# One load's last 20 KB per row, spread unevenly over the DMA engines

## The chip, the cores and the metric

The kernel runs on 1 core of one Trainium2 chip. The metric is the device time of one execution in microseconds, the median of several runs. A profiled execution has its own time, and inside that a span, which reaches from the first to the last instruction of the program that the profile shows.

## The reference

One decode step of a transformer block with modulation from a condition, for a batch of 2 and a single new token. The width is 512, there are 32 heads of 128, and the caches of keys and values hold 4096 positions per head and batch entry, all in fp32. Cut to what is computed:

```python
mod = (silu(c) @ w_mod).reshape(2, 6, 1, -1)        # sa, ca, ga, sb, cb, gb
h = layernorm(x) * (1 + ca) + sa
q = (h @ wq) split into 32 heads
scores = einsum("bhqd,bhkd->bhqk", q, k_cache) * 128 ** -0.5
o = einsum("bhqk,bhkd->bhqd", softmax(scores), v_cache)
x = x + ga * (o @ wo)
h = layernorm(x) * (1 + cb) + sb
x = x + gb * (mish(h @ w1 + b1) @ w2)               # 512 -> 1376 -> 512
```

The two caches are 2 x 32 x 4096 x 128 x 4 bytes each, 268 MB together. All inputs together are a little under 300 MB, and each byte is used once.

## The kernel before

**Layout.** Everything that is read in bulk (keys, values, weights) is laid out beforehand as rows of 128 partitions. One head's keys are `[128, 8192]` floats, 32 KB for each of the 128 rows; one head's values come in two halves of 16 KB per row; a piece of `wq` or `wo` is 8 KB per row. `stream()` packs these pieces in a fixed order into 36 loads, numbered 0 to 35. Loads 1 to 31 are 64 KB per row (`ROW`), 8 MB each, and every one of them holds the keys of the head of the same number. Load 27 holds, in this order in each row: the second half of head 23's values (16 KB), head 27's keys (32 KB), piece 7 of `wq` (8 KB) and piece 5 of `wo` (8 KB). Loads 32 to 35 are smaller and cut into several transfers; the last one, 35, ends with the weights `w2` in four transfers.

**Buffers and queue.** A load goes to one of three buffers named `room`. `load(n)` (line 137) issues load n's transfers on SyncE's queue, at line 143. `used()` issues load n as soon as everything in load n - 3 has been used, so that up to three loads are held or on their way. SyncE's issuing instruction waits for the semaphores of the work that used the buffer; the transfers themselves are queued on the 16 DMA engines behind those issued before. Each transfer has one of eight semaphores in turn.

**Work on a load.** For each head h, VectorE multiplies the keys in place by the query (`products`, line 320, 128x8192) and sums over 128 (`sums`, line 323). A row maximum, an exponential on ScalarE (`soft_max`) and the product with the values on TensorE (`weighted_v`, line 361) follow. `project_q` (line 293) makes the queries of four heads from a piece of `wq`, and `project_o` (line 392) adds four heads' values through a piece of `wo`. The order of these on each engine is the order of the loop over heads: the kernel's schedule is written by hand, and only the waits are put in by the framework.

**The end.** After the loop stand the last heads' values, the attention's output, the second layer norm, `w1`, the activation, and the product with `w2` (line 558) chunk by chunk as `w2` lands. Two VectorE instructions (lines 565 and 566) form `y`, which is stored at line 567.

Of the kernel before, what the change touches and what calls it, by code (L numbers as in the profile page):

```python
# [13 lines left out]
P = 128  # L14
# [11 lines left out]
OUT_STEP = 1  # L26
AHEAD = (14, 22)
ROW = 2 * BIG


def stream():


    order, n_v = [], 0
    for h in range(1, HEADS):
        order.append(("k", h))
        if h % HC == HC - 1 and HC < h < HEADS - 1:
            c = (h + 1) // HC
            order.append([("wq", c), ("wo", c - 2)])
        if h not in AHEAD:  # L40
            order += [("v", n_v, 0), ("v", n_v, 1)]
            n_v += 1
    order = [x if isinstance(x, list) else [x] for x in order]

    def size(x):
        return sum(SIZES[key[0]] for key in x)

    loads = [[([("m01", 0), ("wq", 0), ("wq", 1)], (4 * W,)), ([("k", 0)], (BIG,))]]
    for _ in range(1, HEADS):
        row = []  # L50
        while size(row) < ROW:
            room = ROW - size(row)
            row += order.pop(next(i for i, x in enumerate(order) if size(x) <= room))
        loads.append([(row, (ROW,))])
    last = [("v", h, i) for h in range(HEADS - 4, HEADS) for i in range(2)]
    assert order == [[key] for key in last[:2]], order
    loads += [
        [(last[:2] + [("wo", 6), ("wo", 7), ("m2", 0)], (BIG + 3 * W,))],
        [(last[2:4], (BIG,)), (last[4:6], (BIG,))],
        [([("m4", 0)] + last[6:], (W + HALF, W, W))],  # L60
        [
            ([("m3", 0), ("w1", 0)], (W + 2 * sum(WIDTHS), 2 * sum(WIDTHS))),
            ([("m5", 0), ("w2", 0)], (W + 5 * 512, 4 * 512, 512, 512)),
        ],
    ]
    return loads
# [3 lines left out]
def kernel(  # L70
# [17 lines left out]
    nc = tc.nc  # L88
# [29 lines left out]
    def take(t, keys):  # L118
        lo = 0
        for key in keys:  # L120
            kind, n = key[:2]
            part = t[:, lo : lo + SIZES[kind]]
            lo += SIZES[kind]
            if kind == "k":
                k_t[n] = part.rearrange("p (j d) -> p j d", d=DH)
            elif kind == "v":
                v_t[n, key[2]] = part.rearrange("p (c n) -> p c n", n=512)
            elif kind in ("wq", "wo"):
                (wq_t if kind == "wq" else wo_t)[n] = part.rearrange("p (k n) -> p k n", k=G)
            else:  # L130
                w_t[kind] = part.rearrange("p (k n) -> p k n", k=NCH if kind == "w2" else G)
# [4 lines left out]
    def load(n):  # L136

        t = kvp.tile([P, ROW], F32, tag="room", name=f"room{n}", bufs=3)
        lo = 0
        for keys, srcs in loads[n]:  # L140
            take(t[:, lo:], keys)
            for src in srcs:
                nc.sync.dma_start(out=t[:, lo : lo + src.shape[-1]], in_=src)  # L143
                lo += src.shape[-1]

    loaded = 0

    def used(*keys):

        nonlocal loaded  # L150
        done.update(keys)
        while loaded < len(loads) and (
            loaded < 3 or all(key in done for keys, _ in loads[loaded - 3] for key in keys)
        ):
            load(loaded)
            loaded += 1
# [16 lines left out]
        out=fold, in_=ident.rearrange("p (g r) -> p r g", g=G), axis=AX.X, op=ALU.add  # L173
# [3 lines left out]
        out=mean_w, in0=fold[:, None, :].to_broadcast([P, G, R]), scalar1=1.0 / D, scalar2=None, op0=ALU.mult  # L177
# [4 lines left out]
        out=half, in_=ident.rearrange("p (b r) -> p r b", b=B), axis=AX.X, op=ALU.add  # L182
# [330 lines left out]
    for k in range(G):  # L513
        lo = 0
# [9 lines left out]
    lo = 0  # L524
    for g in reversed(range(G)):
# [3 lines left out]
        lo = hi  # L529
# [41 lines left out]
def _lay_out(np, a):  # L571


    def rows(w):

        return w.reshape(-1, P, w.shape[-1]).transpose(1, 0, 2)

    def q_rows(v):

        return v.reshape(2, 4, P).transpose(1, 0, 2).reshape(8, P)  # L580

    B, H, S, DH = a["A_k_cache"].shape
    kv = {
        kind: a[n].reshape(B, H, P // B, -1).transpose(1, 0, 2, 3).reshape(H, P, -1)
        for kind, n in (("k", "A_k_cache"), ("v", "A_v_cache"))
    }
    wq = rows(a["A_wq"]).reshape(P, 4, 8, 512).transpose(2, 0, 1, 3).reshape(8, P, -1)
    wo = a["A_wo"].reshape(8, 4, P, 512).transpose(0, 2, 1, 3).reshape(8, P, -1)
    wm = rows(a["w_mod"])
    w1 = rows(a["B_w1"])  # L590
    starts = np.cumsum((0,) + WIDTHS)
    b1c = np.zeros((P, 12), a["B_b1"].dtype)
    w2 = np.zeros((P, len(CHUNKS), 512), a["B_w2"].dtype)
    for n, (g, j) in enumerate(CHUNKS):
        f0 = starts[g] + P * j
        f1 = min(f0 + P, starts[g + 1])
        b1c[: f1 - f0, n] = a["B_b1"][f0:f1]
        w2[: f1 - f0, n] = a["B_w2"][f0:f1]

    pieces = {**kv, "wq": wq, "wo": wo, "m01": [wm[:, :, :1024]], "w1": [w1], "w2": [w2]}  # L600
    for n in (2, 3, 4, 5):
        pieces[f"m{n}"] = [wm[:, :, 512 * n : 512 * (n + 1)]]
    def piece(kind, n, part=None):
        row = pieces[kind][n].reshape(P, -1)
        return row if part is None else row[:, HALF * part : HALF * (part + 1)]

    arrays = {
        "head": np.stack([q_rows(a["c"]), q_rows(a["A_x"])], axis=1),
        "b1c": b1c,
    }  # L610
    for n, parts in enumerate(stream()):
        for i, (keys, widths) in enumerate(parts):
            row = np.concatenate([piece(*key) for key in keys], axis=1)
            cuts = np.split(row, np.cumsum(widths)[:-1], axis=1)
            for j, t in enumerate(cuts):
                arrays[f"load{n}_{i}_{j}"] = np.ascontiguousarray(t)
    return arrays

# [27 lines left out]
```

## Time and profile before

| | |
|---|---|
| Time, median of 3 runs | 697.43 us (697.37 to 697.83) |
| The profiled execution's own time | 697.51 us |
| Its span | 695.7 us |
| Mean granted TensorE clock | 0.674 |
| Busy: VectorE, TensorE, ScalarE, GpSimd | 84%, 41%, 6%, 1% |
| DMA packets | 6802, 297.54 MB, mean 428 GB/s |

In the page and the answers of the trace, times are microseconds from the start of the span. PE is TensorE (PEld its weight loads), DVE is VectorE, ACT is ScalarE, POOL is GpSimd and SP is SyncE; a q behind the name means the engine's sequencer. In the view by windows, a row gives for each stretch the busy time and the number of instructions of each engine, then the granted clock, the share of the 16 DMA engines that were busy, and what they moved. A packet's whole time is counted in the window in which it begins, so that a share in a short window can be a little over 1.

### The profile page before, as it was taken

The page shows a single profiled execution, that of the slowest core. Times are in us where ns is not written, and L with a number is a line of the kernel's source. Part 1 is how long each engine was busy: PE and PEld are TensorE (multiplying, and loading weights), DVE is VectorE, ACT ScalarE, POOL GpSimd, SP SyncE. Part 2 cuts the span into 40 slices and gives each one's busy share as a digit, 9 for nine tenths or more (in the row PEclk, how much of TensorE's full clock was granted, in tenths as well). Part 3 has the DMA queues.
Part 4 walks back from the last instruction along what each step waited for, and adds up shares of the span by engine and source line. Part 5 has one row for each costly group of instructions (what it writes and reads, how often), then busy time and mean ns, then how long its engine had stood idle before and what let it go on. Part 6 is the DMA issues. An engine that isn't in the chain of part 4 may idle for free.

```text
span 695.7 us, 3912 instructions
## 1 busy us (share of the span) xinstructions
PE 284.7 (41%) x1636; PEld 103.9 (15%) x1636; DVE 587.5 (84%) x220; ACT 44.0 (6%) x168; POOL 4.2 (1%) x19
## 2 busy tenths in 40 slices
PE   3603334335145624335232806235333515124677
PEld 1201011001012201101100301011101101001235
DVE  3599989999999999999999999999999999899002
ACT  1000000000000000000000000000000010000011
POOL 2000000000000000000000000000000000000000
PEclk9855655669565566556585656666575568556899
DMA  9999999999999999999999999999999999999997
GB/s 387 458 422 422 422 457 445 419 423 430 437 453 422 426 430 427 456 430 419 430 437 452 427 422 426 445 434 437 426 423 442 430 448 427 422 434 423 423 420 297
DMA packets 6802, 297.54 MB, mean 428 GB/s; under 512 B 888, under 2 KB 1024, under 8 KB 1280
## 3 DMA queue, kind: packets, MB, share of 16 engines
q1 hardware_dynamic: 6624, 297.27, 99.1%
q8 instruction: 13, 0.21, 0.1%
q10 hardware_dynamic: 160, 0.01, 0.0%
q14 instruction: 5, 0.04, 0.0%
HBM read 297.22 MB, written 0.07 MB: 427 GB/s over the span
## 4 chain that ended last, share of the span: by engine, by line
DMA 69%; DVE 28%; PE 3%; issue 0%; SPq 0%; ACT 0%; DVEq 0%
DMA room<-in_load 69%; DVE room L320 14%; DVE s L323 14%; PE qps L293 1%; PE ov L361 1%; PE modps L249 1%; PE yps L558 0%; SPq L143 0%; DVE m L336 0%; DVE hcw L282 0%; PE hps L239 0%; ACT q L294 0%; DVE hq L272 0%; DVE hq L273 0%; DVE y L565 0%
## 5 line engine op out<-in xcount | busy, mean ns | idle before, releaser
L320 DVE TENSOR_TENSOR room<-room,q 128x8192 f32<-128x8192 f32 x32 | 278.1, 8691 | 46.8 <-DMA room<-in_load 39.6
L323 DVE TENSOR_REDUCE s<-room 128x64 f32<-128x8192 f32 x32 | 277.9, 8683 | 0.4 <-DVE m L336 0.3
L361 PE MATMUL ov<-room,e 128*32 128x512 f32 x1024 | 174.1, 832 | 74.2 <-ACT e L339 40.4
L332 PE MATMUL mt<-d,same 128*128 128x64 f32 x64 | 19.0, 393 | 200.0 <-DVE d L330 200.0
L361 PEld LDWEIGHTS ov<-room,e 128*32 128x32 f32 x1024 | 39.0, 144 | 181.8 <-issue 128.5
L339 ACT ACTIVATE e<-s,m 64x64 f32<-64x64 f32 x64 | 22.1, 345 | 553.8 <-DVE m L336 553.0
L293 PE MATMUL qps<-room,hcw 128*128 128x512 f32 x64 | 46.1, 891 | 4.8 <-DMA room<-in_load 4.0
L332 PEld LDWEIGHTS mt<-d,same 128*128 128x128 f32 x64 | 13.8, 268 | 228.0 <-DVE d L330 181.1
L347 PE MATMUL l<-l,ones 128*128 128x8 f32 x16 | 4.5, 358 | 76.4 <-ACT e L339 76.4
L384 PE MATMUL otp<-pick,o 128*128 128x8 f32 (+2 forms) x72 | 13.2, 311 | 33.7 <-ACT o L376 32.1
L293 PEld LDWEIGHTS qps<-room,hcw 128*128 128x128 f32 x64 | 17.9, 292 | 27.9 <-issue 21.9
L376 DVE COPY o<-ov 128x256 f32<-128x256 f32 x1 | 0.4, 425 | 24.1 <-ACT o L376 24.1
L384 PEld LDWEIGHTS otp<-pick,o 128*128 128x128 f32 x72 | 12.4, 259 | 42.7 <-ACT o L376 42.6
L347 PEld LDWEIGHTS l<-l,ones 128*128 128x128 f32 x16 | 3.8, 294 | 77.8 <-ACT e L339 77.8
L336 DVE TENSOR_REDUCE m<-mt 128x1 f32<-128x64 f32 x32 | 6.9, 217 | 6.3 <-PE mt L332 6.3
L339 ACT ACTIVATION_READ_ACCUMULATOR e<-s,m 64x1 f32 x64 | 11.8, 185 | 0.0
L392 PE MATMUL att<-room,ot 128*32 128x512 f32 x62 | 9.6, 676 | 5.2 <-DMA room<-in_load 4.7
L330 DVE TENSOR_SCALAR d<-half,m 128x64 f32<-128x64 f32 x32 | 8.1, 254 | 1.1
L249 PE MATMUL modps<-room,ct 128*32 128x128 f32 (+1 forms) x160 | 8.1, 346 | 2.1 <-DMA room<-in_load 2.1
L328 DVE TENSOR_REDUCE m<-s 128x1 f32<-128x64 f32 x32 | 6.9, 217 | 0.9
L376 ACT COPY o<-ov 128x512 f32<-128x512 f32 (+1 forms) x9 | 5.0, 561 | 27.7 <-PE ov L361 27.6
L294 ACT ACTIVATE q<-qps 128x512 f32<-128x512 f32 x8 | 4.8, 597 | 15.9 <-PE qps L293 15.7
(101 smaller groups left out, 61.2 us busy)
## 6 DMA issues: line engine op xcount, KB each, us to landing
room<-in_load SPq DMA_DIRECT2D x4, 4096.0 KB, 25.2
room<-in_load SPq DMA_DIRECT2D x1, 7168.0 KB, 38.9
room<-in_load SPq DMA_DIRECT2D x1, 3072.0 KB, 26.4
room<-in_load SPq DMA_DIRECT2D x3, 1024.0 KB, 28.5
room<-in_load SPq DMA_DIRECT2D x1, 2400.0 KB
room<-in_load SPq DMA_DIRECT2D x1, 2304.0 KB, 20.2
room<-in_load SPq DMA_DIRECT2D x1, 1376.0 KB, 15.6
room<-in_load SPq DMA_DIRECT2D x2, 256.0 KB, 22.6
```

Source lines behind the costliest of these rows:

```text
L249: nc.tensor.matmul(ps[R * g : R * (g + 1)], lhsT=ct[:, k, :], rhs=t[:, k, :].rearrange("p (m n) -> p m n", m=n)[:, :, P * g : P * (g + 1)] ...
L293: nc.tensor.matmul(ps, lhsT=hcw[:, k, :], rhs=wq_t[ch][:, k, :], start=(k == 0), stop=(k == G - 1))
L320: nc.vector.tensor_tensor(out=k_t[h], in0=k_t[h], in1=qv, op=ALU.mult)
L323: nc.vector.tensor_reduce(out=s_t[h], in_=k_t[h], axis=AX.X, op=ALU.add)
L328: nc.vector.tensor_reduce(out=m_t[h][:, 0:1], in_=s_t[h], axis=AX.X, op=ALU.max)
L330: nc.vector.tensor_scalar(out=d, in0=half, scalar1=m_t[h][:, 0:1], scalar2=None, op0=ALU.mult)
L332: nc.tensor.matmul(mps[h], lhsT=same, rhs=d, start=True, stop=True)
L339: nc.scalar.activation(e_t[i][own_b, :, M * i + 4 * b : M * i + 4 * b + 4], s_t[h][own_b].rearrange("p (c m) -> p c m", m=4), AF.Exp, bias ...
L347: nc.tensor.matmul(lps[n], lhsT=ones, rhs=sum_t[n % 2], start=True, stop=True)
L361: nc.tensor.matmul(ov[bank][R * g : R * (g + 1), :], lhsT=e_t[h % HC][:, NB // 2 * part + c, :], rhs=v_t[h, part][:, c, :], start=(first a ...
L384: nc.tensor.matmul(tps[:, x], lhsT=o_t[m], rhs=pick_t[n][:, m, x], start=(m == 0), stop=(m == 3),)
L392: nc.tensor.matmul(att[R * i : R * (i + 1), :], lhsT=ot_t[n % 2][:, i, :], rhs=wo_t[n][:, i, :], start=(n == 0), stop=(n == H // HC - (2 i ...
```

## The change

Load 27 is cut into two parts along each row: the first 44 KB (11264 floats) go as before, one transfer of 128 rows. The last 20 KB (5120 floats: the last 4 KB of head 27's keys, and the pieces of `wq` and `wo`) go as five transfers, all on the same queue and one behind the other:

- rows 0 to 111 in one transfer, 112 = 16 x 7 rows;
- rows 112 to 116, 117 to 121 and 122 to 126, a transfer of five rows each;
- row 127 in one transfer of five pieces of 4 KB, which the source holds as five rows of their own behind the 128 (padded with zeros that no transfer reads).

With seven rows for each of 16 engines in the first of these transfers and one row (or one piece) for each of five engines in the others, five of the 16 DMA engines carry 7 + 3 + 1/5 rows of 20 KB and the eleven others 7, where each carried 8 before. No byte is added or dropped. The instructions of the four computing engines are the same and in the same order; SyncE issues six transfers for load 27 in place of one. The first multiplication on head 27's keys (line 320) now waits for all six, since the last 4 KB of those keys lie in the part that is cut off; so does the projection of the queries at line 293, for the five that bring `wq`.

```diff
+MORE = 27
+PART = 5 * 1024
+EVEN = 112
...
-        loads.append([(row, (ROW,))])
+        loads.append([(row, (ROW - PART, PART) if len(loads) == MORE else (ROW,))])
...
             for src in srcs:
-                nc.sync.dma_start(out=t[:, lo : lo + src.shape[-1]], in_=src)
+                dst = t[:, lo : lo + src.shape[-1]]
                 lo += src.shape[-1]
+                if src.shape[0] == P:
+                    nc.sync.dma_start(out=dst, in_=src)
+                    continue
+                nc.sync.dma_start(out=dst[:EVEN], in_=src[:EVEN])
+                for r in range(EVEN, P - 1, 5):
+                    nc.sync.dma_start(out=dst[r : r + 5], in_=src[r : r + 5])
+                nc.sync.dma_start(
+                    out=dst[P - 1 :].rearrange("p (a b) -> p a b", a=5), in_=src[None, P:, : PART // 5]
+                )
...
+                if n == MORE and j:
+                    last = np.zeros((5, PART), t.dtype)
+                    last[:, : PART // 5] = t[-1].reshape(5, -1)
+                    t = np.concatenate([t, last])
                 arrays[f"load{n}_{i}_{j}"] = np.ascontiguousarray(t)
```

## The prediction

> **What bounds the kernel now.** I read the page first: its DMA queues (packets, MB, share of 16 engines), and the chain of work that ended last.
>
> ```profile
> span 695.7 us, 3912 instructions
> ...
> q1 hardware_dynamic: 6624, 297.27, 99.1%
> q8 instruction: 13, 0.21, 0.1%
> ...
> q14 instruction: 5, 0.04, 0.0%
> ...
> DMA 69%; DVE 28%; PE 3%; issue 0%; SPq 0%; ACT 0%; DVEq 0%
> ```
>
> The loads alone (q1) fill 99.1% of 16 engines' span. The kernel is bound by moving its bytes; VectorE's 28% of the chain is where the chain runs through the work that frees a buffer, while transfers already queued go on. The rate of one engine follows from the q1 row: 297.27 MB in 0.991 x 16 x 695.7 = 11,031 engine-us, 26.95 KB per us (thousands of bytes). A row of 20 KB (20,480 B) takes one engine 0.76 us.
>
> Can all 16 be always full and yet something be won? Only where they don't finish together. The view by windows at the end shows that:
>
> ```profile
> core 0: us, PE busy (x) PEld busy (x) DVE busy (x) ACT busy (x) POOL busy (x), PEclk, DMA share, GB/s
> ...
> 688.50:689.00 0.50, 0.00 (x0) 0.00 (x0) 0.05 (x1) 0.00 (x0) 0.00 (x0) 1.00 0.98 389
> 689.00:689.50 0.50, 0.24 (x9) 0.27 (x13) 0.00 (x0) 0.00 (x0) 0.00 (x0) 1.00 0.76 299
> 689.50:690.00 0.50, 0.50 (x28) 0.50 (x23) 0.00 (x0) 0.00 (x0) 0.00 (x0) 1.00 0.71 283
> 690.00:690.50 0.50, 0.50 (x29) 0.50 (x23) 0.10 (x1) 0.00 (x0) 0.00 (x0) 1.00 0.61 238
> 690.50:691.00 0.50, 0.50 (x28) 0.50 (x21) 0.19 (x1) 0.00 (x0) 0.00 (x0) 1.00 0.40 156
> 691.00:691.50 0.50, 0.43 (x16) 0.16 (x8) 0.00 (x0) 0.00 (x0) 0.00 (x0) 1.00 0.27 102
> 691.50:692.00 0.50, 0.34 (x12) 0.34 (x16) 0.00 (x0) 0.00 (x0) 0.00 (x0) 1.00 0.27 102
> 692.00:692.50 0.50, 0.50 (x28) 0.50 (x24) 0.00 (x0) 0.00 (x0) 0.00 (x0) 1.00 0.19 70
> ```
>
> Times 16, the share is the number of engines still at work: all at 688.75, about eleven at 689.75, six at 690.75, four at 691.5, three at 692.25. Every engine gets the same rows from the loads, so the unequal finish must have another cause; apart from some KB at the start and the store at the end, the only other traffic is that of the instruction queues q8 and q14, 18 packets in all, 13 of them of 0.21 MB / 13 = 16 KB. They can't be spread evenly over 16 engines. So about five engines lead, by some 3.0 us (done at about 689.4, the last ones at about 692.4), seven come between, and four are last.
>
> That the last engines set the end shows in the tail of the chain:
>
> ```profile
> 669.27 22.34 DMA room<-in_load
> 691.61 0.04 issue
> 691.66 1.30 PE yps L558 x40
> 692.96 0.02 issue
> 692.97 0.47 PE yps L558 x8
> ```
>
> PE takes the chunks of w2 as they land (691.61, and again just before 692.97), and behind the last landing lies a fixed tail of 695.7 - 692.9 = 2.8 us. Whatever moves the slowest engine's last landing moves the end by as much. The sum is made against the profiled execution, 697.51 us with its span of 695.7; the median, 697.43, is 0.08 lower, so changes carry over as they stand.
>
> **The change, part by part.** What it does to the bytes: eleven engines lose one 20 KB row, -0.76 us; five get 10.2 rows for 8, 2.2 x 0.76 = +1.67 us. If nothing else happened and the five are those that lead by 3.0 us, they end 1.3 us ahead of the old end, the last ones 0.76 us ahead of it: a gain of 0.76 us at the very most, 0.11%. About 0.2% (1.4 us) is what a measurement of this kernel can tell from no change. A gain that could be told has no source in this change, since no engine that is last now loses more than one row.
>
> [...]
>
> What it adds on SyncE: five more issues.
>
> ```profile
> L143 SPq DMA_DIRECT2D room<-in_load x45: 327/328/533, 0.7 to 670.2; - x45
> L143 SPq EVENT_SEMAPHORE  x36: 17/17522/20702, 13.0 to 662.2; - x36
> ...
> DMA to landing us min/median/max: 12.2/40.5/59.3
> ```
>
> Each takes 0.33 to 0.53 us, 2.7 us at most, and SyncE stands 17.5 us (median) at its waits before the next load. Median time to landing is 40.5 us, of which a load's own transfer is half (8.39 MB at 16 x 26.95 KB per us is 19.5 us), so another whole load is queued ahead: free. Were that cover gone, the price would be the 2.7 us. Smaller packets: the view by windows gives the rate on the rows of 64 KB around load 27's last third, and on the rows of 8 to 32 KB later.
>
> ```profile
> 540.00:550.00 10.00, 3.28 (x5) 1.67 (x6) 8.60 (x4) 0.00 (x0) 0.00 (x0) 0.50 0.99 426
> 550.00:560.00 10.00, 7.36 (x34) 2.89 (x36) 10.00 (x3) 2.12 (x7) 0.00 (x0) 0.82 0.98 426
> ...
> 650.00:660.00 10.00, 5.60 (x34) 1.45 (x34) 0.57 (x3) 0.88 (x4) 0.00 (x0) 0.83 0.99 424
> ```
>
> 426 against 424: 0.5% at most, on the third of one load that is cut off (8 x 0.76 = 6.1 us) 0.03 us. I take 0.
>
> The added wait: L320 for head 27, and behind it everything on VectorE, stands until all six transfers are in. Before, it waited like this:
>
> ```profile
> 506.50 40.87 DMA room<-in_load
> 547.36 0.02 issue
> 547.39 8.69 DVE room L320
> ...
> 564.88 0.02 SPq L143
> ```
>
> And by the view of waits (us in total, times, longest):
>
> ```profile
> DVE room L320 <- DMA room<-in_load: 39.6, 29, 2.5
> ```
>
> VectorE already waits for DMA 1.4 us a head (39.6 / 29), so it follows the loads and nothing else; a load's last row later by x makes it x later once, and the next issue (load 30, at 564.88 before) by x, against the queued load of 19.5 us. It costs nothing at the end by itself.
>
> Now the part with no row of its own: **five engines writing five neighbouring rows at the same time.** Every bulk transfer of the trace has 128 rows, eight for each engine, and all engines run together at one flat rate of 26.95 KB per us. That flat rate can be the engine's own, or that of a way into SBUF which each engine has to itself as long as all 128 rows are written, eight rows to a way. The trace can't part the two, because in it they coincide. In the first case a five-row transfer takes 0.76 us and the sum is the one above. In the second, neighbours share a way that is already full with the next load's rows of the engine to which it belongs (DMA share 0.98 and 0.99 in the two windows above). Bounds: no sharing, 0; all five rows and that engine on one way, each at a sixth of the rate, 6 x 0.76 - 0.76 = 3.8 us per transfer, 11.4 us for three (the fourth, 4 KB pieces of one row, is a fifth of that and lies within the rounding). The value that I take is the middle, 5.7 us, since eight rows to a way mean that five neighbours are more likely to sit on one or two ways than on five. The five engines then end 1.67 + 5.7 = 7.4 us later than before. Their lead covers 3.0, and the end moves by +4.4 us: 697.43 + 4.4 = 701.8. They don't catch up, because from there to the end their queue is never empty. The 112-row transfer could suffer too, if an engine's seven rows are not among its usual eight; bounded by a doubling, 7 x 0.76 = 5.3 us; I take 0, by the 128-row loads, the nearest rows, and leave it to the upper part of the range.
>
> [...]
>
> **The rivals.** *The balance comes out.* The rate is the engine's own, the leading five are the right ones: -0.76 us, 696.7. For it: the share of about eleven at 689.75 means just five that have finished, and five are loaded. [...] The five have 3.0 - 1.67 = 1.33 us to spare: it holds as long as the three transfers together lose less than that, 0.44 us each, and turns to a loss that can be told at 1.33 + 1.4 = 2.7 us, 0.9 us each. *The wrong five.* No view names an engine. If one of the five is among the last four, it ends 1.67 us later: 699.1; if it is among the middle seven (about 1.5 us behind the leaders), it ends where the old last one did, at about 697.5. *A gain that shows,* below 696.0, needs something that I don't see; it is left for the unknown.
>
> **How the numbers follow.** Shared ways 0.60, balance 0.27, wrong five 0.08 (half of it slower by over 0.2%), unknown gain 0.05. Slower 0.60 + 0.04 = 0.64; same 0.27 + 0.04 = 0.31; faster 0.05. The time is that of the likeliest, 701.8. Its own range goes from 699.0, where it begins to be told, to 697.43 + 11.4 + 1.67 - 3.0 = 707.5. The range of all goes from the balance, with 0.1 us to spare, 696.6, to 706.5, which leaves out the very end of the bound and the unknown gain.
>
> **What would show it.** In the windows at 540 to 560 us the share should stay near 1 while the GB/s fall below the 426 of before, since packets that share a way take longer without the engines' standing idle. L320 for head 27 should start at about 553, not 547.4, and VectorE should wait for DMA that much longer, once. At the end, the taper should be turned round: eleven engines done early, and five alone at the last, a share of about 0.3 for some us before a last landing near 697. The forecast is wrong if the share falls from 1 to 0 within some 2.5 us and the tail of the chain stands where it was or 0.8 us earlier; then the rate is the engine's own. If the taper is long, but VectorE's wait at head 27 is not, the five are the wrong ones.

## The result, and the profile after

The kernel with the change takes 708.11 us (median of four runs, 707.67 to 708.99); the kernel before took 697.4 us on the same chip (697.37 to 697.83). The ratio is 1.0154, 95% interval 1.0136 to 1.0171: slower by 10.7 us. The forecast was 701.8 us with a range up to 706.5; the direction is right, the size is not. One run of one kernel below, `r112_16`, took 742.56 us in a slower state than all the others and is left out of every figure.

The page of the profile after (rows of the span, of the GB/s in 40 slices of 17.7 us, of the load queue and of the chain):

```profile
span 706.3 us, 3925 instructions
...
GB/s 387 445 416 464 427 413 434 453 417 423 461 419 427 442 434 420 431 453 417 434 449 423 428 449 423 419 439 445 419 425 332 331 423 438 443 415 424 424 419 264
...
q1 hardware_dynamic: 6792, 297.27, 98.9%
...
DMA 62%; DVE 33%; PE 3%; another core or an unknown queue 2%; issue 0%; SPq 0%; ACT 0%; DVEq 0%
```

The same 297.27 MB move in a span that is 10.6 us longer, and yet the queue's packets fill 98.9% of 16 engines' time, where they filled 99.1%. So the engines didn't stand idle: packets took longer. Two slices show where, 332 and 331, from 529.7 to 565.0 us. The view by windows there, in the columns of before (the last three are the clock, the share of the DMA engines and GB/s):

```profile
540.00:550.00 10.00, 0.69 (x2) 0.50 (x2) 5.71 (x3) 0.00 (x0) 0.00 (x0) 0.50 1.05 225
550.00:560.00 10.00, 0.30 (x1) 0.33 (x2) 0.41 (x1) 0.00 (x0) 0.00 (x0) 0.50 1.01 315
560.00:570.00 10.00, 7.57 (x24) 2.46 (x23) 10.00 (x3) 1.44 (x6) 0.00 (x0) 0.78 0.96 415
```

225 and 315 GB/s at a share of 1, where 426 stood twice. At 560 us it is over. VectorE's timeline for the multiplications of heads 27 and 28 (start, busy time, and in brackets the idle time before it and what ended it; line 320 of before is line 332 here), and the view of waits:

```profile
559.59 8.69 DVE L332 TENSOR_TENSOR room<-room,q 128x8192 f32<-128x8192 f32 x1 [13.80 <-DMA room<-in_load]
...
578.48 8.69 DVE L332 TENSOR_TENSOR room<-room,q 128x8192 f32<-128x8192 f32 x1 [0.87 <-DMA room<-in_load]
```

```profile
DVE room L332 <- DMA room<-in_load: 50.1, 29, 13.8
```

Head 27 starts 12.2 us later than before (559.59 for 547.39), with one wait of 13.8 us; head 28 waits 0.87 us, no longer than the three heads before 27 (1.0 to 1.4 us). In the chain of waits the same stretch has another name:

```profile
545.53 0.25 DVE d L342
545.78 13.51 another core or an unknown queue
...
559.59 8.69 DVE room L332
```

That piece is the 2% of the page's "another core or an unknown queue". With one core there is no other: VectorE's timeline above names the transfers of a load (`room<-in_load`) for the same idle time. The end, by windows:

```profile
699.50:700.00 0.50, 0.13 (x5) 0.16 (x9) 0.00 (x0) 0.00 (x0) 0.00 (x0) 1.00 0.52 197
700.00:700.50 0.50, 0.50 (x24) 0.50 (x23) 0.00 (x0) 0.00 (x0) 0.00 (x0) 1.00 0.33 123
700.50:701.00 0.50, 0.50 (x29) 0.50 (x22) 0.00 (x0) 0.00 (x0) 0.00 (x0) 1.00 0.13 53
701.00:701.50 0.50, 0.50 (x28) 0.50 (x22) 0.29 (x1) 0.00 (x0) 0.00 (x0) 1.00 0.08 33
...
702.00:702.50 0.50, 0.28 (x11) 0.24 (x12) 0.00 (x0) 0.00 (x0) 0.00 (x0) 1.00 0.07 25
...
703.00:703.50 0.50, 0.50 (x23) 0.29 (x12) 0.00 (x0) 0.00 (x0) 0.00 (x0) 1.00 0.14 33
```

Half of the engines are at work at 699.75 us (0.52); before, that stood between 690.25 (0.61) and 690.75 (0.40). So the middle of the taper moved by some 9 us: not only the five, but the engines that were to carry less are late. From 701 us on about one engine is alone (0.08 x 16 = 1.3). The tail of the chain follows the last landing, as before:

```profile
679.62 22.60 DMA room<-in_load
702.22 0.04 issue
702.27 1.30 PE yps L570 x40
703.57 0.02 issue
703.59 0.47 PE yps L570 x8
```

703.57 for 692.96: the last landing moved by 10.6 us and the end with it.

### The profile page after: what moved, and what is told of

The parts are those of the page before. It is cut to its first block, busy times and chain, and to the rows that moved or that the text cites. A ratio compares the mean times of both kernels' runs of the same rounds, so it can differ in the third digit from the quotient of the medians.

```text
span 706.3 us, 3925 instructions
## 1 busy us (share of the span) xinstructions
PE 285.1 (40%) x1636; PEld 105.1 (15%) x1636; DVE 587.5 (83%) x220; ACT 44.0 (6%) x168; POOL 4.2 (1%) x19
## 3 DMA queue, kind: packets, MB, share of 16 engines
q1 hardware_dynamic: 6792, 297.27, 98.9%
## 4 chain that ended last, share of the span: by engine, by line
DMA 62%; DVE 33%; PE 3%; another core or an unknown queue 2%; issue 0%; SPq 0%; ACT 0%; DVEq 0%
DMA room<-in_load 62%; DVE room L332 16%; DVE s L335 16%; PE qps L305 1%; PE ov L373 1%; PE modps L261 1%; PE yps L570 0%; SPq L149 0%; DVE m L348 0%; DVE d L342 0%; DVE hcw L294 0%; DVE m L340 0%; ACT q L306 0%; PE hps L251 0%
## 5 line engine op out<-in xcount | busy, mean ns | idle before, releaser
L396 PE MATMUL otp<-pick,o 128*128 128x8 f32 (+2 forms) x72 | 13.8, 319 | 35.9 <-ACT o L388 34.6
```

Source lines behind the costliest of these rows:

```text
L396: nc.tensor.matmul(tps[:, x], lhsT=o_t[m], rhs=pick_t[n][:, m, x], start=(m == 0), stop=(m == 3),)
```

## The experiments

The theory on record was that neighbouring rows share a way, so that the five-row transfers delay the five engines; its rivals were an engine's own rate (bytes alone), and the wrong five. The ways are the author's supposition (theory W below): the runs show how long packets take by the rows that are written, and none shows a way itself. After the result a third thing stood open: whether the 112-row transfer, priced at nothing, was slow too. Two families of kernels part them. Each run's ratio is against the kernel before, run on the same chip (697.42 to 697.52 us).

### The cut and its transfers of 16 engines

These start from the kernel before, cut load 27 as the change does, and bring the 20 KB in transfers of 128, 112, 64 or 16 rows, all multiples of 16, so that every engine is meant to get the same eight rows' worth (in the trace after, by its packets, the 112 rows went seven to each engine):

```diff
+MORE = 27
+PART = 5 * 1024
+PIECES = [(0, 128, 1)]                         # cut: first row, end, step
-        loads.append([(row, (ROW,))])
+        loads.append([(row, (ROW - PART, PART) if len(loads) == MORE else (ROW,))])
...
-                nc.sync.dma_start(out=t[:, lo : lo + src.shape[-1]], in_=src)
+                dst = t[:, lo : lo + src.shape[-1]]
+                for first, end, step in PIECES if n == MORE and src.shape[-1] == PART else [(0, P, 1)]:
+                    nc.sync.dma_start(out=dst[first:end:step], in_=src[first:end:step])
```

**The cut alone** (`cut`).

> Load 27 in two transfers of 128 rows, 44 KB and 20 KB wide: the cut alone, no other shape and no uneven split. Theory W (the rows of SBUF are reached over 16 ways, each as fast as one engine; a transfer of 128 rows gives every engine a way of its own, every other shape makes engines share): no change, 697.4 within 0.5 us, packets of 20 KB take 0.76 us. Theory T (a transfer costs by being small or cut off, wherever its rows lie): up to 1 us slower.

697.58 us, ratio 1.0002 (0.9992 to 1.0012). Its 20 KB packets took 0.76 to 0.77 us each (here and below, the times of single packets are from the trace's packet records). Windows:

```profile
540.00:560.00 20.00, 9.95 (x34) 4.92 (x34) 18.44 (x6) 1.95 (x6) 0.00 (x0) 0.67 1.05 452
```

No dip: the cut, the smaller packets and the added wait cost nothing.

**112 rows and 16 rows** (`r112_16`), without a five-row transfer.

```diff
+PIECES = [(0, 112, 1), (112, 128, 1)]
```

> The 20 KB as rows 0 to 111 and rows 112 to 127, so that every engine carries 7 + 1 = 8 rows as before: no uneven split and no five-row transfer. If the five-row transfers were the cost, as the prediction priced it, 697.4. [...]

705.98 us (median of three runs, 705.06 to 706.51), ratio 1.0121 (1.0104 to 1.0138).

```profile
540.00:560.00 20.00, 4.11 (x6) 2.01 (x7) 9.36 (x4) 0.00 (x0) 0.00 (x0) 0.50 1.00 261
```

With no engine meant to carry more than another and no five-row transfer, about 8.5 of the 10.7 us are there: 261 GB/s at a share of 1.00, the median 20 KB packet takes 1.50 us for 0.77.

**Eight transfers of 16 neighbouring rows** (`next16`).

```diff
+PIECES = [(0, 16, 1), (16, 32, 1), (32, 48, 1), (48, 64, 1), (64, 80, 1), (80, 96, 1), (96, 112, 1), (112, 128, 1)]
```

> The 20 KB as eight transfers of 16 neighbouring rows, one row for each engine in each. [...] Theory T: eight transfers cost the same here as with rows 8 apart.

711.45 us, ratio 1.0201 (1.0185 to 1.0216).

```profile
540.00:560.00 20.00, 0.69 (x2) 0.50 (x2) 5.87 (x3) 0.00 (x0) 0.00 (x0) 0.50 1.03 186
```

The slowest, with a median packet of 2.06 us, 2.7 times the usual. One such transfer costs about (711.45 - 697.58) / 8 = 1.7 us, so that of the 8.4 us between `r112_16` and `cut` some 6.7 belong to the 112 rows, if the two add up.

**Eight transfers of every eighth row** (`step16`).

```diff
+PIECES = [(0, 128, 8), (1, 128, 8), (2, 128, 8), (3, 128, 8), (4, 128, 8), (5, 128, 8), (6, 128, 8), (7, 128, 8)]
```

> The same eight transfers of 16 rows, one row for each engine, but each of every eighth row of 128. [...] Theory T: the same time as with neighbouring rows.

705.54 us, ratio 1.012 (1.0105 to 1.0135).

```profile
540.00:560.00 20.00, 4.68 (x7) 2.35 (x8) 9.94 (x4) 0.00 (x0) 0.00 (x0) 0.50 1.00 283
```

Spreading the same 16 rows over all partitions brings the median packet from 2.06 to 1.55 us and the loss from 13.9 to 8.0 us. Which rows are written together decides, not the number of transfers, which is eight in both: theory T, with the same time for the two, is out.

**Two halves of 64 rows** (`half64`).

```diff
+PIECES = [(0, 64, 1), (64, 128, 1)]
```

> The 20 KB as rows 0 to 63 and rows 64 to 127, four rows for each of 16 engines in each transfer. Theory W: 64 rows of one half lie on eight of the 16 ways, so two engines on each: 1.5 us a packet, 8 x 0.76 = 6 us slower, 703.5. Theory T: two transfers in place of one, under 1 us.

705.48 us, ratio 1.0116 (1.0101 to 1.0131).

```profile
540.00:560.00 20.00, 4.96 (x8) 2.40 (x9) 10.11 (x4) 0.00 (x0) 0.00 (x0) 0.51 1.00 281
```

Even two even halves double the packets (1.55 us, 1.55 / 0.77 = 2.0). The expectation had 1.5 us from two engines on a way; the time agrees, and the sharing itself is not shown. The 16 rows of `step16` have the same 1.55 us, the 16 neighbours of `next16` 2.06 us.

### Five engines by themselves, behind load 34

The other family leaves all loads of before as they are and appends three transfers of five rows of 20 KB behind load 34, into columns that nothing uses; load 35 follows as before, and what the three bring is never read. Five engines carry 3 x 0.76 = 2.28 us more, in rows that are chosen:

```diff
+EXTRA = [(112, 117, 1), (117, 122, 1), (122, 127, 1)]      # x_neigh
+WIDE = 5120
...
+        if n == 34:
+            spare, src = t[:, ROW - WIDE :], loads[1][0][1][0][:, :WIDE]
+            for first, end, step in EXTRA:
+                nc.sync.dma_start(out=spare[first:end:step], in_=src[first:end:step])
```

**The change's neighbouring rows** (`x_neigh`).

> The kernel before, and behind load 34 three transfers of five rows of 20 KB (rows 112 to 126, into columns of that buffer that nothing reads, the bytes read twice): five engines carry 3 rows more, 2.28 us, the other eleven what they had. Nothing else is cut. If the five lead by 3.0 us and share no way, no change. [...]

703.81 us, ratio 1.0091 (1.0074 to 1.0108); packets 1.23 to 2.22 us.

**Rows four apart, from 0** (`x_own`).

```diff
+EXTRA = [(0, 20, 4), (1, 20, 4), (2, 20, 4)]
```

> The same three extra transfers of five rows, but rows 0, 4, 8, 12, 16 and so on, four apart. [...] By the lead of 3.0 us no change, 697.4; if the slowest of the five leads by only 1.1 us, 698.6. Theory T: the same time as with neighbouring rows.

698.49 us, ratio 1.0015 (1.0006 to 1.0024); all 15 packets 0.76 to 0.77 us. The same bytes, again on five engines, cost 1.0 us here and 6.3 us there.

**Rows four apart, from 64** (`x_far`).

```diff
+EXTRA = [(64, 84, 4), (65, 84, 4), (66, 84, 4)]
```

> The same three extra transfers of five rows, four apart, but in the other half of the rows: 64, 68, 72, 76, 80 and so on. [...] Theory T: the same as the other two.

702.88 us, ratio 1.0083 (1.0066 to 1.01); packets 0.99 to 1.58 us, most of them 1.5. The rows lie four apart as in `x_own`, and yet they lose 5.4 us (702.88 for 697.46 of the kernel before) where those lose 1.0: the distance between the rows doesn't decide alone.

The three in one window, after the row of before:

```profile
670.00:680.00 10.00, 8.33 (x103) 4.47 (x95) 1.77 (x8) 1.40 (x4) 0.42 (x1) 1.00 1.02 427
```

`x_neigh`:

```profile
670.00:680.00 10.00, 5.34 (x46) 1.36 (x38) 0.00 (x0) 0.58 (x1) 0.00 (x0) 0.79 1.04 253
```

`x_own`:

```profile
670.00:680.00 10.00, 8.36 (x104) 4.59 (x96) 1.81 (x8) 1.40 (x4) 0.42 (x1) 1.00 1.02 428
```

`x_far`:

```profile
670.00:680.00 10.00, 8.10 (x59) 3.15 (x59) 0.42 (x1) 1.13 (x3) 0.08 (x1) 0.83 1.04 275
```

The share is above 1 in all; what the engines move falls from 427 to 253 and 275 GB/s, and stays at 428 in `x_own`.

**Is it the reading or the writing?** `x_own_src` writes rows four apart and reads the neighbouring ones, `x_neigh_src` the other way round (in each pair of triples the first is written, the second read):

```diff
+EXTRA = [((0, 20, 4), (112, 117, 1)), ((1, 20, 4), (117, 122, 1)), ((2, 20, 4), (122, 127, 1))]  # x_own_src: written, read
+EXTRA = [((112, 117, 1), (0, 20, 4)), ((117, 122, 1), (1, 20, 4)), ((122, 127, 1), (2, 20, 4))]  # x_neigh_src
```

> The extra transfers of five rows into rows four apart (0, 4, 8, 12, 16 and so on), but read from five neighbouring rows of the source (112 to 116 and so on). Theory W (the cost lies where the rows are written): as with rows four apart on both sides, 698.5, packets 0.76 us. Theory R (it lies where they are read from): as with neighbouring rows on both sides, 703.8, packets 1.2 to 2.2 us.

> The reverse: written to neighbouring rows (112 to 116 and so on), read from rows four apart (0, 4, 8, 12, 16). Theory W: 703.8, packets 1.2 to 2.2 us. Theory R: 698.5, packets 0.76 us.

698.53 us, ratio 1.0015 (1.0006 to 1.0024), and 703.23 us, ratio 1.0082 (1.0066 to 1.0099). First `x_own_src`, then `x_neigh_src`:

```profile
670.00:680.00 10.00, 9.43 (x101) 4.54 (x100) 1.01 (x4) 1.53 (x5) 0.42 (x1) 0.83 1.02 427
```

```profile
670.00:680.00 10.00, 5.07 (x43) 1.17 (x35) 0.00 (x0) 0.63 (x2) 0.00 (x0) 0.75 1.03 252
```

The rows that are written decide. For the transfers of 112, 64 and 16 rows the two sides were not exchanged.

**Rows four apart, from 32** (`x_own32`).

```diff
+EXTRA = [(32, 52, 4), (33, 52, 4), (34, 52, 4)]
```

> The extra transfers of five rows into rows 32, 36, 40, 44, 48 and so on, 32 above those of the kernel that cost nothing but its bytes. [...] Theory W with ways of eight neighbouring rows: 32, 36 and 40, 44 lie in pairs on one way each, beside another engine's rows: about 702, packets 1.5 us or more.

698.67 us, ratio 1.0016 (1.0007 to 1.0026), packets 0.76 to 0.77 us.

```profile
670.00:680.00 10.00, 8.14 (x100) 4.30 (x92) 1.81 (x8) 1.40 (x4) 0.42 (x1) 1.00 1.01 425
```

Rows 32 to 50 are as free as rows 0 to 18 (698.67 and 698.49 us, packets of 0.76 to 0.77 us in both), and rows 64 to 82 are not (702.88 us, most packets 1.5 us). Ways of eight neighbouring rows, by which about 702 us and 1.5 us were expected here, are ruled out.

**One extra transfer in its own rows** (`x_own1`), for the lead of the five:

```diff
+EXTRA = [(0, 20, 4)]
```

> One of the three extra transfers into rows 0, 4, 8, 12, 16: 0.76 us more for each of the five engines. If three of them cost 1.07 us because the slowest of the five leads by 2.28 - 1.07 = 1.2 us, one costs nothing: 697.4 within 0.3. If the cost is that of issuing, a third of it: 697.8.

697.55 us, ratio 1.0000 (0.999 to 1.0009). 0.76 us more on each of the five costs nothing, 2.28 us cost about 1.0: the slowest of the five leads the last engine by at least 0.76 us and by about 2.28 - 1.0 = 1.2 to 1.3 us, not by 3.0. The taper of `x_own` shows it:

```profile
693.00:693.50 0.50, 0.50 (x24) 0.50 (x20) 0.00 (x0) 0.00 (x0) 0.00 (x0) 1.00 0.07 25
693.50:694.00 0.50, 0.50 (x24) 0.35 (x16) 0.00 (x0) 0.00 (x0) 0.00 (x0) 1.00 0.17 37
```

0.07 of 16 is one engine, alone from 693 us on. Five with equal leads would end together, at 0.3.

Of theory W's expectations, `cut` (697.4), `x_own_src` (698.5) and `x_neigh_src` (703.8) came out within 0.6 us; `half64` came out 2.0 us above its 703.5. The theory leaves out the rows of other transfers: in the four kernels of the first family that lost time, 8 or 9 rows of the 44 KB part and 17 or 18 of load 28 were slowed too, in `cut` one and none.

## Why the prediction was right in its direction and wrong in its size

The last engine of the kernel after can be followed through its packets, since each begins within some ns of the end of the one before on the same engine. That is an inference from their times, as no view names the engine. In it:

```
                                       forecast     after
bytes, 2.2 rows x 0.76                   +1.67      +1.67
seven rows of the 112-row transfer        0         +5.4    (10.7 us for 5.3)
three five-row transfers                 +5.7       +2.65   (4.9 us for 2.27)
last row of the 44 KB part                0         +1.6
4 KB piece, first row of load 28          0         +0.6
lead of the five                         -3.0       -1.2    (from x_own)
sum                                      +4.4      +10.7    (measured +10.7)
```

- **The step that failed is the 112-row transfer, taken at 0.** The prediction gave it the bound of a doubling, 5.3 us, and then the value of the 128-row loads as the nearest rows. But by the prediction's own theory, eight rows to a way, those loads are the one case without sharing, so they could not price a transfer of another number of rows. The bound was the value: in the kernel after, 127 packets of 20 KB have a median of 1.47 us, and `r112_16` shows the loss without any five-row transfer. In the kernel after itself, 48 rows began and ended between 542.2 and 548.0 us, when nothing but the 112-row transfer was under way, and took 1.32 to 1.56 us each. All 16 engines paid it, which is why the whole taper moved: even the first engine to end load 28 did so at 571.96 us, for 563.95 before.
- **The five-row transfers, 5.7 us,** were about right as a number: `x_neigh` less `x_own` is 703.81 - 698.49 = 5.3 us. They were not right in kind, and that the number fits is luck: the forecast put the delay into the three rows of the five engines. In `x_neigh` three median packets (1.84 us) lose only 3 x (1.84 - 0.76) = 3.2 us; the rest must be lost in rows that were under way beside them, which took 2.5 to 2.7 times their usual time at 674.0 us. In the kernel after, the last engine lost 2.65 us in its three. No run shows the shared way from which the 5.7 us was worked out; what the runs show is the time of the packets by the rows written, 1.23 to 2.22 us in rows 112 to 126 (`x_neigh`) and 0.76 to 0.77 us in rows 0 to 18, four apart (`x_own`).
- **The rows under way beside these transfers** were not priced. The slowed stretch takes them in: 8 rows of the 44 KB part took up to 3.25 us (usually 1.67), and 36 rows of load 28 up to 5.42 us (usually 2.42). Some 2.2 us of it fall on the last engine.
- **The lead, 3.0 us,** is true of the five engines that finish first, but they are not the five that were loaded. In the packets of the kernel after, the five began their last row of the 44 KB part 0, 0.03, 0.12, 0.63 and 2.05 us behind the first of the 16: the fifth of them was the last of all. `x_own1` and `x_own` put the lead of the slowest at 1.2 us. This is the rival of the wrong five, in part. The bytes alone, 1.67 - 1.2, would have cost 0.5 us (an estimate), which could hardly be told.
- **That the balance comes out,** the first rival, is ruled out by `x_neigh`, `x_far` and `r112_16`. Five extra rows at a time cost nothing but their bytes in rows 0 to 18 and 32 to 50, four apart (`x_own` 698.49 us, `x_own32` 698.67 us). Whether all of load 27's last 20 KB could be written so, with the right five loaded, no run shows.
- **Right:** 0.76 us a row (0.76 to 0.77 in `cut`); five more issues, the small packets and the added wait at nothing (`cut`, and SPq 0% of the chain after); a share near 1 with fewer GB/s at 540 to 560 us; VectorE's single long wait at head 27, though to 559.59 and not 553; no catching up, since the last landing and the end moved together. The split came out as intended: by the packets of the trace after five of the 16 engines carry ten rows of 20 KB and a 4 KB piece and the eleven others seven.
- **The taper** is turned round only at its very end: one engine alone for two us (0.08 and 0.07), where five at 0.3 were forecast, because the eleven others were late as well.

## To carry to other kernels

Before work is moved between DMA engines, ask for each transfer which rows its engines write at the same moment: here only transfers of all 128 rows, and those of five rows four apart among rows 0 to 18 or 32 to 50, ran at the full rate (0.76 to 0.77 us for 20 KB), and transfers of 112, 64 or 16 rows about halved it or worse (medians of 1.47 to 2.06 us). A share of the DMA engines near 1 doesn't say that they work at their rate (1.05 at 225 GB/s above); read GB/s beside it. And where a forecast rests on a mechanism, put every transfer through it, not only the one that looks odd.

## What the runs showed of the hardware that was not expected

- **The other engines slow down too, not only the five that carry the extra rows.** In `x_far`, of the load and extra rows under way at 674.0 us, four of them extra, none is at its rate: the load rows take 2.0 to 2.1 times what rows of their size take otherwise, and at 677.75 us, with two extra rows left, still 1.8 to 2.0 times. In `x_neigh` they take 2.5 to 2.7 times at 674.0 us. When the last extra row is in, the rows return to 1.0. So in these two traces every load row slows for as long as such rows are being written. Why is not shown: `x_own_src` and `x_neigh_src` tell the rows written from the rows read (698.53 and 703.23 us), and no run goes further.
- **Two halves are no better than every eighth row** (`half64` and `step16`, both 1.55 us), and 16 neighbours take 2.06 us (`next16`), 2.7 times the 0.77 us of all 128 rows. What makes it 2.0 times in the one case and 2.7 in the other no run shows.
- **The uneven finish has its cause in the instruction queue's packets, as far as the times tell.** In the kernel before, all 16 engines end a load within 0.5 us of each other up to 80 us. Behind the first 16 KB packet of the instruction queue q8, at 94.5 us, one of them ends 1.7 us after the first; at 658 us, after ten such packets, the spread is 3.35 us. Each of them took about 1.07 us, and the load packet behind it some 0.5 us longer, 1.55 us in all; the 13 seem to go round eight engines, so that some are delayed twice. This is read from the packets' times and wasn't tried.
